# Ten direct pairs instead of eleven, and the transform's work staged around them

## The chip, the cores and the metric

The kernel runs on one core of a Trainium2 chip. The metric is device time in microseconds (us), and for the kernel before it is 1369.09 us, the median of three runs (1367.53 to 1373.18).

## The reference, cut to what matters

```python
S, D, Df = 2048, 576, 4608          # one sequence, all float32
x = A_x
g = sigmoid((x * gate_w).sum(-1, keepdims=True))            # one gate per token
X = rfft2(x); a = irfft2(X * (w_r + 1j * w_i), s=(S, D))    # over tokens and features
h = gelu(x @ w_gate) * (x @ w_up)                           # 576 -> 4608, tanh form
b = h @ w_down                                              # 4608 -> 576
return g * a + (1 - g) * b
```

Both branches work on the same x. All is float32: a product is made of three reduced-precision products (high by high, low by high, high by low parts).

## The kernel before, in words

**The dense branch sets the pace on TensorE (PE).** The 2048 tokens are two halves of 1024. The hidden width 4608 is 36 blocks of 128, two of which make a pair, so there are 18 pairs for each half, 36 in all. The string `PLAN` (L35) has one letter for each. A pair "c" (`conv`) is direct: for two hidden blocks, two groups of 512 tokens, gate and up, `chain` (L826) issues 14 matmuls of 512 columns, 8 x 14 = 112 in all. A pair "s" (`products`) takes its four output blocks from seven block products (Strassen's way), each for gate and up: `seven` (L1140) issues 7 matmuls of 512 columns, 7 x 2 x 7 = 98. Both are followed by the same 96 matmuls of 288 columns of the down projection (`down_mm`, L898), 12 for each of 8 token groups.

An "s" pair needs sums of blocks of x (`operands`, tiles `sx`, `xhi`, `xlo` and the third weight buffer `gu_72`) and sums of weight blocks (`total`, L1120, DVE L1128). Each of its weights is copied rounded by ScalarE (ACT, `copy`, L218), and the rest of it is made by VectorE (DVE, L1111). The first product's result is copied into a second bank of PSUM by ACT, `copy(ps[1][s], v)` in `products`, and the second product is added there: so the second product waits for those two copies.

PSUM has three kinds of banks, two of each: `pgu` and `pone` for the 512-column results and `pdn` for the down projection. `bank` (L844) chooses by a counter, `turns`, which starts at 0: two chains take `pone`, then two `pgu`, and so on. The very first two chains (`first_chains`, L849) always take both `pone`.

**The transform branch** is a generator, `spectral` (L652). Its work is put between matmuls: after each chain or product `gap` (L727) lets it emit as many DVE instructions as the PE time issued since then pays for. Every engine executes its own list strictly in the order of emission. So what stands early in DVE's list and waits for a transfer holds up what stands behind it, though that may be wanted by PE.

The stages are: operands for the first "s" phase; the feature transforms of half one (`forward_rows`, in the tile `rows`, 128 x 5120), stored to DRAM as `fw`, and of half two, both during the first "s" pairs; during the direct pairs the token transform, in the tile `til`, which is the same memory as `sx` (hence the direct pairs): moves from rows to tiles, a stage over tiles (`first_tiles`, with factors), 16 column blocks (`columns`, with 192 matmuls of 290 columns, L283, and exchanges of half tiles by DMA, `hx` and `til`, L269 to L273), and the inverse stage (`last_tiles`); then `operands` again; then during the second "s" phase the inverse feature transforms (`inverse_rows`) whose results are added to the output in DRAM (`yd`). At the end of the direct pairs half one is moved to rows directly (`into_rows`) and half two is stored to DRAM (`bw`) and fetched later (`fetch`, `fetched_rows`). A pair that begins an "s" phase waits until the operands are done; the last pair of all waits until the generator is.

Gates: `gate_sum` (L754) sums x times gate_w, `release` (L949) scales the first four results, which wait in `til`, by one minus the gate.

All SyncE (SP) DMAs stand in one list too.

Of the kernel before, what the change touches and what calls it, by code (L numbers as in the profile page):

```python
# [34 lines left out]
PLAN = "c" * 2 + "s" * 10 + "c" * 11 + "s" * 13  # L35
# [126 lines left out]
def _build(nc, tc, a):  # L162
    with ExitStack() as ctx:
# [42 lines left out]
        bw = dram.tile([P, 8 * SW], F32, name="bw", tag="bw")  # L206
# [32 lines left out]
        def columns():  # L239
# [3 lines left out]
            ww = [[b[:, SW * i:SW * (i + 1)] for i in range(2)] for b in (tmp[:, SW:3 * SW], misc)]  # L243
# [153 lines left out]
        def first_tiles(h):  # L397
            T = tiles()
            sp = tmp[:, 0:2 * SW].rearrange("p (e k) -> p e k", e=2)
            tmps = [tmp[:, SW * i:SW * (i + 1)] for i in range(4)]  # L400
            tmps = [(x, x[:, 0:NK], x[:, NK:]) for x in tmps]
            e = slice(2 * h, 2 * h + 2)
            yield from _butterfly(vec, lambda i: T[:, i, e], lambda i: T[:, i, e, re], lambda i: T[:, i, e, im],
                                  TAKEN, sp, -1, (1.28, 0.69))
# [5 lines left out]
        def last_tiles():  # L410
            T = tiles()
            rows = rows_tile()
            sp = rows[:, 0:4 * SW].rearrange("p (e k) -> p e k", e=4)
            tmps = [rows[:, SW * i:SW * (i + 1)] for i in range(4, 8)]
            tmps = [(x, x[:, 0:NK], x[:, NK:]) for x in tmps]
            places = [((k, LEFT[o]), o * k) for k in range(1, 4) for o in range(1, 4)]
# [3 lines left out]
            yield from _butterfly(vec, lambda i: T[:, i], lambda i: T[:, i, :, re], lambda i: T[:, i, :, im],  # L420
                                  range(4), sp, 1, (2.5, 1.28))
# [164 lines left out]
        def load_rows(rows, h):  # L586
            v = rows.rearrange("p (c g k) -> p c g k", c=2, g=4)
            nc.sync.dma_start(v[:, 0], a["xn"][h, :, :, 0:OW])
            nc.sync.dma_start(v[:, 1, :, 0:2 * D - OW], a["xn"][h, :, :, OW:])
            pl.memset(v[:, 1, :, 2 * D - OW:], 0.0)  # L590

        def with_gates(work):
# [6 lines left out]
            for v in work:  # L599
                yield v  # L600
                n += 1
                t = n // 10 - 1
                if n % 10 == 0 and t < 8:
# [16 lines left out]
        def fetch(b):  # L620
            for i, o in enumerate(spots_of[b]):
                g, c = divmod(i, 2)
                t = 4 * b + 2 * g
                nc.sync.dma_start(o, bw.rearrange("p (t c k) -> p t c k", t=8, c=2)[:, t:t + 2, c])

        def fetched_rows():

            rows = rows_tile()
# [3 lines left out]
            for b in range(2):  # L632
                for i, x in enumerate(spots_of[b]):
# [7 lines left out]
                if b == 0:  # L641
                    yield None
                    fetch(1)
# [5 lines left out]
        pairs_of += [misc[:, 0:SW], misc[:, SW:]]  # L649
        spots_of = [[x.rearrange("p (t k) -> p t k", t=2) for x in pairs_of]] * 2  # L650

        def spectral(rows):  # L652
            for i in (2, 1):
                load_part(0, i)
            for _ in range(2):
                yield None
            yield from operands(0)
            yield from with_gates(forward_rows(0, rows))
# [820 lines left out]
```

## Time and profile before

| | |
|---|---|
| median, lowest and highest of 3 runs | 1369.09, 1367.53, 1373.18 us |
| the profiled execution's own time | 1368.03 us |
| its span in the trace | 1366.1 us |
| PE, DVE, ACT, POOL busy | 1344.1, 1104.2, 833.0, 264.5 us |
| matmuls | 7364 |

The span runs from the first to the last instruction of the trace; 1.9 us of the profiled execution lie outside it. Times in the timeline are from the span's start. [...] In rows of the timeline the bracket at the end is the idle time of the engine before that row and what ended it.

### The profile page before, as it was taken

The page shows a single profiled execution, that of the slowest core. Times are in us where ns is not written, and L with a number is a line of the kernel's source. Part 1 is how long each engine was busy: PE and PEld are TensorE (multiplying, and loading weights), DVE is VectorE, ACT ScalarE, POOL GpSimd, SP SyncE. Part 2 cuts the span into 40 slices and gives each one's busy share as a digit, 9 for nine tenths or more (in the row PEclk, how much of TensorE's full clock was granted, in tenths as well). Part 3 has the DMA queues.
Part 4 walks back from the last instruction along what each step waited for, and adds up shares of the span by engine and source line. Part 5 has one row for each costly group of instructions (what it writes and reads, how often), then busy time and mean ns, then how long its engine had stood idle before and what let it go on. Part 6 is the DMA issues. An engine that isn't in the chain of part 4 may idle for free.

```text
span 1366.1 us, 19980 instructions
## 1 busy us (share of the span) xinstructions
PE 1344.1 (98%) x7364; PEld 1185.5 (87%) x7364; DVE 1104.2 (81%) x1543; ACT 833.0 (61%) x1428; POOL 264.5 (19%) x323
## 2 busy tenths in 40 slices
PE   8999999999999999999999999999999999999998
PEld 6878888888888888898888888878888888888887
DVE  6689989959999878768688587379999579999654
ACT  4676676656665544555566537556766776676672
POOL 0011212212212212222120122111222322221231
PEclk9999999999999999999999999999999999999999
DMA  8556766787667967999996687556767796676897
GB/s 303 186 126 156 146 127 125 149 229 137 127 120 157 196 128 176 200 226 237 259 243 208 178 181 165 88 137 125 133 130 130 137 225 124 126 140 128 148 215 175
DMA packets 107921, 226.92 MB, mean 166 GB/s; under 512 B 12720, under 2 KB 25008, under 8 KB 107696
## 3 DMA queue, kind: packets, MB, share of 16 engines
q0 software_dynamic: 44928, 90.98, 44.4%
q1 hardware_dynamic: 62896, 134.68, 30.5%
q8 instruction: 57, 0.93, 0.3%
q14 instruction: 40, 0.33, 0.1%
HBM read 121.46 MB, written 97.01 MB: 160 GB/s over the span
## 4 chain that ended last, share of the span: by engine, by line
PE 79%; DMA 8%; DVE 7%; ACT 3%; issue 2%; SPq 1%; DVEq 0%; ACTq 0%
PE pdn L906 27%; PE pgu L1146 5%; PE pone L1146 5%; PE pgu L1148 5%; PE pgu L1147 5%; PE pone L1148 5%; PE pone L1147 5%; PE pgu L831 3%; PE pgu L833 3%; PE pgu L832 3%; DMA hx<-til 3%; PE pgu L1149 2%; PE pone L1149 2%; PE pone L831 2%; PE pone L833 2%
## 5 line engine op out<-in xcount | busy, mean ns | idle before, releaser
L919 POOL DMA_DIRECT2D yd<-stg x264 | 229.6, 871 | 1029.7 <-ACT stg L931 838.4
L906 PE MATMUL pdn<-dn,hb 128*128 128x288 f32 x2508 | 364.9, 295 | 1.4 <-DVE dn L810 1.0
L906 PEld LDWEIGHTS pdn<-dn,hb 128*128 128x128 f32 x2508 | 352.3, 188 | 13.9 <-DVE dn L810 1.2
L931 ACT ACTIVATE stg<-pdn,omg 128x576 f32<-128x576 f32 x276 | 204.0, 740 | 246.3 <-PE pdn L906 241.8
L218 ACT ACTIVATE gu<-wq 64x256 fp32r<-64x256 f32 (+4 forms) x353 | 230.1, 666 | 92.2 <-DVE gu L1111 58.7
L1111 DVE TENSOR_TENSOR gu<-wq,gu 128x768 fp32r<-128x768 f32 x161 | 153.6, 955 | 39.9 <-ACT gu L218 37.1
L906 PE MATMUL pdn<-dn,hx 128*128 128x288 f32 x924 | 142.9, 295 | 0.5 <-DVE wq L970 0.2
L906 PEld LDWEIGHTS pdn<-dn,hx 128*128 128x128 f32 x924 | 132.1, 188 | 4.9 <-DVE wq L970 0.5
L831 PE MATMUL pgu<-xhi,gu 128*128 128x512 f32 x296 | 115.9, 392 | 1.2 <-DVE gl L888 1.2
L833 PE MATMUL pgu<-xlo,gu 128*128 128x512 f32 x296 | 115.8, 391 | 0.0
L832 PE MATMUL pgu<-xhi,gu 128*128 128x512 f32 x296 | 115.6, 390 | 0.0
L1128 DVE TENSOR_TENSOR wq<-wq 128x768 f32<-128x768 f32 x92 | 87.5, 953 | 5.0 <-ACT gu L218 4.8
L218 ACT ACTIVATE hb<-gl 128x512 fp32r<-128x512 f32 x68 | 42.7, 628 | 55.5 <-DVE gl L888 53.3
L833 PEld LDWEIGHTS pgu<-xlo,gu 128*128 128x128 f32 x296 | 55.6, 188 | 12.6 <-DVE xlo L776 0.4
L831 PEld LDWEIGHTS pgu<-xhi,gu 128*128 128x128 f32 x296 | 55.6, 188 | 11.6 <-DVE gl L888 1.9
L832 PEld LDWEIGHTS pgu<-xhi,gu 128*128 128x128 f32 x296 | 55.6, 188 | 9.6
L810 DVE TENSOR_TENSOR dn<-wq,dn 128x576 fp32r<-128x576 f32 x72 | 54.4, 756 | 7.6 <-ACT dn L218 7.5
L888 DVE TENSOR_TENSOR gl<-gl,pgu 128x512 f32<-128x512 f32 x37 | 25.3, 684 | 42.5 <-PE pgu L838 42.3
L1146 PE MATMUL pgu<-xhi,gu 128*128 128x512 f32 x140 | 55.6, 397 | 2.6 <-ACT pgu L218 2.6
L1146 PE MATMUL pone<-xhi,gu 128*128 128x512 f32 x136 | 54.1, 398 | 3.1 <-ACT pone L218 3.0
L1146 PE MATMUL pgu<-sx,gu 128*128 128x512 f32 x140 | 55.0, 393 | 1.7 <-DVE gl L1167 1.7
L1147 PE MATMUL pgu<-xhi,gu 128*128 128x512 f32 x140 | 55.2, 394 | 0.0
(242 smaller groups left out, 2844.9 us busy)
## 6 DMA issues: line engine op xcount, KB each, us to landing
yd<-stg POOLq DMA_DIRECT2D x264, 288.0 KB, 4.9
wq<-ws SPq DMA_DIRECT2D x92, 384.0 KB, 4.4
wq<-wd SPq DMA_DIRECT2D x72, 288.0 KB, 5.0
wq<-wgu SPq DMA_DIRECT2D x24, 640.0 KB, 6.1
colm<-col POOLq DMA_DIRECT2D x32, 256.0 KB, 6.4
tmp<-wf SPq DMA_DIRECT2D x16, 290.0 KB, 6.5
hx<-til SPq DMA_DIRECT2D x64, 72.5 KB, 5.8
til<-hx SPq DMA_DIRECT2D x64, 72.5 KB, 3.6
```

The lines of the kernel that those rows point to most:

```text
L218: act.activation(o, i, AF.Copy)
L831: pe.matmul(ps, w[:, 0, k, c], xhi[tb][:, k], start=k == 0, stop=False)
L832: pe.matmul(ps, w[:, 1, k, c], xhi[tb][:, k], start=False, stop=False)
L833: pe.matmul(ps, w[:, 0, k, c], xlo[tb][:, k], start=False, stop=False)
L906: pe.matmul(ps[half], h[:, l, c], d[:, k, half * HD:(half + 1) * HD], start=part == 0 and n == 0, stop=part == 1 and n == 2)
L919: pl.dma_start(yd[u], o, accum_op=ALU.add)
L931: put(u, lambda o: act.activation(o.rearrange("p (c k) -> p c k", c=2), v[:, :, 0:HD], AF.Copy, scale=omg[:, u:u + 1]), i == 0)
L1111: vec.tensor_tensor(o, x.rearrange("p (c k) -> p c k", c=3), f(w[:, 256:1024]).rearrange("p (c k) -> p c k", c=3), ALU.subtract)
L1128: at(lead, lambda: vec.tensor_tensor(o, u, v, ALU.subtract))
L1146: pe.matmul(ps, hi, xh[:, t], start=start and t == 0, stop=False, skip_group_check=True)
L1147: pe.matmul(ps, lo, xh[:, t], start=False, stop=False, skip_group_check=True)
L1148: pe.matmul(ps, hi, xl[:, t], start=False, stop=False, skip_group_check=True)
```

## The change

- The third letter group of `PLAN` goes from 11 to 10 "c" pairs and the last from 13 to 14 "s".
- `turns` starts at 1, so the first `chain` takes a `pgu` bank.
- `total` of an "s" phase's first two weight sums is emitted five gaps after the first weights of that phase, not at the end of the last direct pair.
- At the start 9 idle matmuls instead of 6, the first cast of x ahead of the first weight remainder; the first half of the second weight block is loaded ahead of `msk`, and `sgn` later. The eight gate sums of half one go two to a gap, and `spectral` starts with the releases, after its first loads.
- Half two's rows for the transform come as nine blocks (`xm`): six are loaded into small tiles while half one is transformed (`ahead`), three into `rows` later. The store of `fw` is two DMAs instead of four.
- `first_tiles` and `last_tiles` are cut (two parts, two halves); the column stage's first exchanges are issued between the parts.
- Both halves of the inverse go to DRAM (`bw`, twice as large) and come back by `fetch` and `fetched_rows`; `into_rows` isn't called.

```diff
-PLAN = "c" * 2 + "s" * 10 + "c" * 11 + "s" * 13
+PLAN = "c" * 2 + "s" * 10 + "c" * 10 + "s" * 14
...
             yield from four(0, TAKEN, sp, -1)
+            load_ww(0)
+            yield None
+            for kb in range(2):
+                corner(kb, 0, False)
+            n = 0
+            for v in first_tiles(0, 1):
+                yield v
+                n += 1
+                if n == 10:
+                    for kb in range(2):
+                        corner(kb, 0, True)
+            cols[0] = True
             side.append(beside())
-            load_ww(0)
-            for back in range(2):
-                for kb in range(2):
-                    corner(kb, 0, back)
-                for _ in range(4):
-                    yield None
...
-        def forward_rows(h, rows):
+        def forward_rows(rows, src=None):
             x = blocks(rows, ROW_BLOCK)
+            src = src or x
...
-                yield from nine(((tA, q, 1, s), (q, q, -1, s), (s, p, 1, tA), (p, tA, -0.5, p)))
+                u, v, w = src[i], src[i + 3], src[i + 6]
+                yield from nine(((tA, v, 1, w), (q, v, -1, w), (s, u, 1, tA), (p, tA, -0.5, u)))
...
+        ahead = [misc[:, 0:TB], misc[:, SW:SW + TB], out_rows[3][:, 0:TB], tmp[:, 1536:2048], tmp[:, 2048:2560], gl[1]]
+        def load_block(o, i):
+            nc.sync.dma_start(o, a["xm"][:, i].rearrange("p (g w) -> p g w", g=4))
...
-        def fetched_rows():
+        def fetched_rows(h):
+            for _ in range(5 if h == 0 else 0):
+                yield None
...
-            for b in range(2):
-                for i, x in enumerate(spots_of[b]):
+            for b in range(1 if h == 0 else 2):
+                for i, x in enumerate(places_of[h]):
...
         def spectral(rows):
             for i in (2, 1):
                 load_part(0, i)
-            for _ in range(2):
+            for u in range(4):
+                while len(kept_rows) <= u:
+                    yield None
+                release(u)
                 yield None
...
-            yield from quarters(lambda c: nc.sync.dma_start(fw[:, c], rows[:, c]))
-            for _ in range(2):
+            for c in range(2):
+                nc.sync.dma_start(fw[:, 2 * UNIT * c:2 * UNIT * (c + 1)], rows[:, 2 * UNIT * c:2 * UNIT * (c + 1)])
+            for _ in range(4):
                 yield None
             rows = rows_tile()
-            load_rows(rows, 1)
-            for _ in range(6):
-                yield None
-            yield from forward_rows(1, rows)
+            src = [None] * 9
+            for o, i in zip(ahead, (0, 3, 6, 1, 4, 7)):
+                src[i] = o
+            for i in (5, 2, 8):
+                load_block(x[i], i)
+                src[i] = x[i]
+            yield None
+            yield None
+            yield from forward_rows(rows, src)
...
-            yield from last_tiles()
-            yield None
-            for i in range(4):
-                c = slice(2 * SW * i, 2 * SW * (i + 1))
-                nc.sync.dma_start(bw[:, c], til[0][:, 8 * SW:][:, c])
-                yield None
-            yield from into_rows(0)
-            yield from operands(1)
+            yield from last_tiles(1)
+            yield from with_stores(last_tiles(0), kept(1))
+            yield from with_stores(operands(1), kept(0))
             yield from until(3)
-            fetch(0)
+            fetch(0, 0, places_of[0])
+            yield from fetched_rows(0)
             yield from inverse_rows(0)
-            yield from fetched_rows()
+            yield from fetched_rows(1)
             yield from inverse_rows(1)
...
-        turns = [0]
+        turns = [1]
...
                     prep_b(q + 1, 0)
                     prep_b(q + 1, 1, 2)
+                    at(5, lambda: [total(q + 1, 0), total(q + 1, 1)])
...
-                if tb == 1 and last:
-                    total(q + 1, 0)
-                    total(q + 1, 1)
...
-        for _ in range(6):
+        for _ in range(9):
             pe.matmul(ps, idle[:, 0:P], idle, start=True, stop=True)
```

How the order on the engines moves, at three places.

PE, at the start, from the end of the first two chains (before, then after; `pone` and `pgu` are the PSUM banks that are written):

```order
L857 MATMUL pone<-xlo_65,gu_71 128x512 x2
L857 MATMUL pone<-xtl_67,gu_71 128x512 x4
L831 MATMUL pone<-xhi_63,gu_72 128x512
L832 MATMUL pone<-xhi_63,gu_72 128x512
L833 MATMUL pone<-xlo_65,gu_72 128x512
```

```order
L903 MATMUL pone<-xlo_65,gu_71 128x512 x2
L903 MATMUL pone<-xtl_67,gu_71 128x512 x4
L877 MATMUL pgu<-xhi_63,gu_72 128x512
L878 MATMUL pgu<-xhi_63,gu_72 128x512
L879 MATMUL pgu<-xlo_65,gu_72 128x512
```

The third chain no longer writes a bank that the first two chains have just filled.

DVE, around the start of the second "s" phase (`gl_83<-gl_83,pgu` is gate times up of the last direct chain, `hb` the remainder of its rounding, `wq<-wq 128x768` the weight sums, `gu` the weights' remainders):

```order
L1111 TENSOR_TENSOR gu_70<-wq,gu_70 128x3x256 x2
L888 TENSOR_TENSOR gl_83<-gl_83,pgu 128x512
L892 TENSOR_TENSOR hb_78<-gl_83,hb_78 128x512
L1128 TENSOR_TENSOR wq<-wq 128x768 x2
L1111 TENSOR_TENSOR gu_71<-wq,gu_71 128x3x256
L96 TENSOR_TENSOR tmp<-rows 128x1280
```

```order
L1160 TENSOR_TENSOR gu_71<-wq,gu_71 128x3x256 x2
L1177 TENSOR_TENSOR wq<-wq 128x768 x2
L934 TENSOR_TENSOR gl_83<-gl_83,pgu 128x512
L938 TENSOR_TENSOR hb_78<-gl_83,hb_78 128x512
L1160 TENSOR_TENSOR gu_70<-wq,gu_70 128x3x256
L1177 TENSOR_TENSOR wq<-wq 128x768
```

The two weight sums stand ahead of the last chain's results instead of behind them.

DVE, at the first instructions of half two's forward transform (`tmp` and `rows` of lines 437 to 441, and 446 to 450 of the changed kernel, are the transform; the others serve the "s" pairs):

```order
L1111 TENSOR_TENSOR gu_70<-wq,gu_70 128x3x256
L437 TENSOR_TENSOR tmp<-rows 128x512
L439 TENSOR_TENSOR rows<-rows 128x4x128
L1128 TENSOR_TENSOR wq<-wq 128x768
L437 TENSOR_TENSOR rows<-rows,tmp 128x4x128
L441 SCALAR_TENSOR_TENSOR rows<-tmp,rows 128x4x128
```

```order
L1233 TENSOR_TENSOR xraw<-xraw,pgu 128x512
L446 TENSOR_TENSOR tmp<-misc,orow 128x512
L448 TENSOR_TENSOR rows<-misc,orow 128x4x128
L1233 TENSOR_TENSOR xraw<-xraw,pgu 128x512
L1160 TENSOR_TENSOR gu_71<-wq,gu_71 128x3x256
L446 TENSOR_TENSOR rows<-misc,tmp 128x4x128
L450 SCALAR_TENSOR_TENSOR rows<-tmp,misc 128x4x128
```

The first of these read small tiles that were loaded ahead, not `rows`.

More of the change, by code (lines that the diff above doesn't have):

```diff
@@ L242, in columns @@
             vs = tmp[:, 0:SW]
-            ww = [[b[:, SW * i:SW * (i + 1)] for i in range(2)] for b in (tmp[:, SW:3 * SW], misc)]
+            ww = [[b[:, SW * i:SW * (i + 1)] for i in range(2)] for b in (misc, tmp[:, SW:3 * SW])]
             turn = [d + 4 * q for d in range(4) for q in range(4)]
@@ L692, in spectral, with kept, with_stores @@
             load_xs(1)
-            yield from last_tiles()
-            yield None
-            for i in range(4):
-                c = slice(2 * SW * i, 2 * SW * (i + 1))
-                nc.sync.dma_start(bw[:, c], til[0][:, 8 * SW:][:, c])
-                yield None
-            yield from into_rows(0)
-            yield from operands(1)
+            def kept(h):
+                yield None
+                for i in range(4):
+                    c = slice(8 * SW * h + 2 * SW * (3 - i), 8 * SW * h + 2 * SW * (4 - i))
+                    nc.sync.dma_start(bw[:, c], til[0][:, c])
+                    yield None
+            def with_stores(work, stores):
+                for n, v in enumerate(work):
+                    if n % 2:
+                        next(stores, None)
+                    yield v
+                yield from stores
+            yield from last_tiles(1)
+            yield from with_stores(last_tiles(0), kept(1))
+            yield from with_stores(operands(1), kept(0))
             yield from until(3)
-            fetch(0)
+            fetch(0, 0, places_of[0])
+            yield from fetched_rows(0)
             yield from inverse_rows(0)
-            yield from fetched_rows()
+            yield from fetched_rows(1)
             yield from inverse_rows(1)
@@ L1345, in _build @@
         one, fin = gate_part(0, rows0, gwb)
-        for t in range(8):
-            aux.append(lambda t=t: one(t))
+        for t in range(0, 8, 2):
+            aux.append(lambda t=t: [one(t), one(t + 1)])
         aux.append(fin)
-        for u in range(0, 4, 2):
-            aux.append(lambda u=u: [release(u), release(u + 1)])
         aux.append(lambda: gens.append(spectral(rows0)))
```

87 lines of the change are left out of this document (52 added, 35 removed).

## The prediction, made before the changed kernel was run

> **What bounds the kernel now.** I read the page's busy times first, then the list of waits of PE, then PE's timeline and the windows around each wait.
>
> ```profile
> PE 1344.1 (98%) x7364; PEld 1185.5 (87%) x7364; DVE 1104.2 (81%) x1543; ACT 833.0 (61%) x1428; POOL 264.5 (19%) x323
> ...
> 893.08 0.39 PE L1147 MATMUL pgu<-xhi,gu 128*128 128x512 f32 x1
> ...
> 895.80 0.39 PE L1149 MATMUL pgu<-sx,gu 128*128 128x512 f32 x1
> ```
>
> PE is busy 98% of the span, and from 893.08 to 895.80 there are 12 steps of one matmul each: 2.72 / 12 = 0.227 us. That is the pace of a 512-column matmul when nothing is waited for. So time can come from two places alone: fewer matmuls, or shorter waits of PE. These are its waits:
>
> ```profile
> PE pone L1146 <- ACT pone L218: 3.0, 1, 3.0
> PE pgu L1146 <- ACT pgu L218: 2.6, 1, 2.6
> PE pone L831 <- ACT gl L878: 2.3, 1, 2.3
> PE pgu L1146 <- DVE gl L1167: 1.7, 1, 1.7
> PE pgu L831 <- DVE gl L888: 1.2, 1, 1.2
> PE pone L283 <- ACT til L218: 1.1, 1, 1.1
> PE pone L283 <- DVE colm L276: 0.9, 1, 0.9
> ```
>
> These seven are 12.8 us; no other inside the span's first and last few us is above 1.0. The three longest cost more than they show, because the clock goes down behind them:
>
> ```profile
> 12.00:15.38 3.38, 1.53 (x7) 0.94 (x5) 2.38 (x4) 2.85 (x5) 0.00 (x0) 1.00 1.03 367
> 15.38:18.80 3.41, 2.98 (x7) 2.41 (x8) 2.20 (x4) 2.05 (x4) 0.00 (x0) 0.54 1.01 346
> 83.65:87.06 3.41, 0.81 (x4) 0.35 (x2) 3.38 (x6) 3.09 (x6) 0.00 (x0) 1.00 0.69 152
> 87.06:90.47 3.41, 3.38 (x8) 2.65 (x9) 3.38 (x6) 0.94 (x3) 0.00 (x0) 0.54 0.00 1
> 896.02:899.43 3.41, 0.40 (x2) 0.23 (x2) 2.42 (x3) 2.34 (x4) 0.00 (x0) 1.00 0.67 227
> 899.43:902.85 3.41, 3.41 (x10) 2.61 (x10) 3.41 (x4) 1.15 (x4) 0.00 (x0) 0.54 0.00 0
> ...
> 300.00:310.00 10.00, 8.27 (x43) 6.83 (x42) 9.48 (x14) 5.90 (x10) 1.03 (x2) 1.00 0.51 106
> ```
>
> The first number after the comma is PE's busy time, the third from the end the granted clock. In three stretches of 3.4 us PE works for 1.53, 0.81 and 0.40 us, and in the stretch behind each the clock is 0.54. The wait of 1.7 us near 305 (last row) left it at 1.00.
>
> [...]
>
> **The change, part by part.**
>
> *One direct pair less.* 112 matmuls of 512 columns become 98: 14 x 0.227 = **3.2 us less**. The down projection and the 192 column matmuls stay. The planner inserts no idle gap for a late operand in the changed program, so all of it should be seen.
>
> *The third chain's bank.*
>
> ```profile
> 12.46 1.07 PE L857 MATMUL pone<-xtl,gu 128*128 128x512 f32 x4
> 15.81 0.79 PE L831 MATMUL pone<-xhi,gu 128*128 128x512 f32 x1 [2.28 <-ACT gl L878]
> ...
> 12.09 0.74 ACT L218 ACTIVATE gu<-wq 128x640 fp32r<-128x640 f32 x1 [1.53 <-DMA wq<-wgu]
> ...
> 13.94 1.33 ACT L218 ACTIVATE xhi<-til 128x512 fp32r<-128x512 f32 x2 [0.16 <-DMA til<-xt]
> 15.18 0.58 ACT L878 ACTIVATE gl<-pone 128x512 f32<-128x512 f32 x1
> ```
>
> PE waited for the Gelu that empties `pone`; the Gelu stood behind two copies of x that waited for DMA. With a `pgu` bank the chain needs only weights that were ready at 12.83 (12.09 + 0.74). The wait of 2.28 goes. So does the half clock: in the window of 0.54 seven matmuls ran from 15.81 to 18.80, where 2.99 / 0.227 = 13 fit, so 6 x 0.227 = 1.4 are lost there. Together **3.7 us less**. Bounds: 0 if the next group of tokens is late in its place; 3.7 if nothing is. I take 3.7, because x's copies end at 15.27 and the two chains between take 28 x 0.227 = 6.4 us from 13.5.
>
> *Nine idle matmuls.*
>
> ```profile
> 1.46 2.93 PE L1322 MATMUL pgu<-hb 128*128 128x512 f32 x6 [1.46 <-DVE gate L1318]
> 5.22 2.04 PE L857 MATMUL pone<-xhi,gu 128*128 128x512 f32 x4 [0.84 <-DVE xhi L1329]
> ```
>
> At about 0.45 us each, three more fill the 0.84 us of waiting and add 0.5 to it, while the cast of x moves forward by one DVE instruction (0.42). Bounds +0.5, and -1.0 if the clock rises sooner: the four matmuls at 5.22 take twice the 1.07 of those at 12.46. I take -0.3.
>
> *The weight sums, sooner.* Here the second "s" phase starts:
>
> ```profile
> 893.06 0.69 DVE L888 TENSOR_TENSOR gl<-gl,pgu 128x512 f32<-128x512 f32 x1 [2.33 <-PE pgu L838]
> 894.45 0.69 DVE L892 TENSOR_TENSOR hb<-gl,hb 128x512 fp32r<-128x512 f32 x1 [0.70 <-ACT hb L218]
> 895.05 1.94 DVE L1128 TENSOR_TENSOR wq<-wq 128x768 f32<-128x768 f32 x2
> ...
> 893.78 0.63 ACT L218 ACTIVATE hb<-gl 128x512 fp32r<-128x512 f32 x1 [2.57 <-DVE gl L888]
> 897.09 1.58 ACT L218 ACTIVATE gu<-wq 128x768 fp32r<-128x768 f32 x2 [2.68 <-DVE wq L1128]
> 898.57 1.06 ACT L218 ACTIVATE pone<-pgu 128x512 f32<-128x512 f32 x2
> ...
> 899.20 0.50 PE L1146 MATMUL pone<-xhi,gu 128*128 128x512 f32 x1 [3.01 <-ACT pone L218]
> ...
> 903.20 0.39 PE L1146 MATMUL pone<-xhi,gu 128*128 128x512 f32 x1
> ```
>
> PE wants the copies `pone<-pgu`. In ACT's list they stand behind two weight copies, which wait 2.68 us for the sums, and the sums stand in DVE's list behind the last chain's results. With the sums ahead of L888 (the order on DVE shows it, and DVE was idle for 2.33 us there) ACT goes on at 894.41: two weight copies (1.58) to 895.99, the first PSUM copy (half of 1.06) to 896.5. PE is through with its 14 matmuls at 895.80 + 0.23 = 896.03, so 0.5 remains of 3.01. From 899.20 to 903.20 are ten steps, 4.00 us where 2.27 would do: 1.7 for the clock. Together 2.5 + 1.7 = **4.2 us less**. Bounds: 0, and 4.7.
>
> The first "s" start is the same with another cause:
>
> ```profile
> 83.76 0.68 DVE L888 TENSOR_TENSOR gl<-gl,pgu 128x512 f32<-128x512 f32 x1
> ...
> 80.90 0.39 PE L838 MATMUL pgu<-xtl,gu 128*128 128x512 f32 x1
> ...
> 84.47 0.63 ACT L218 ACTIVATE hb<-gl 128x512 fp32r<-128x512 f32 x1 [0.32 <-DVE gl L888]
> ```
>
> The chain ended at 81.29, but DVE came to its result at 83.76, 2.5 us late, behind work on operands that ACT had finished late; the 2.6 us of PE's wait are that. In the changed order the sums stay ahead of L888, so the early sums don't help here. What does are the operands: their loads go before the releases, the gate sums take half the gaps, and the planner has them done two gaps before the pair, where it had to force one gap at the pair's start. Two gaps are two chain parts of 7 matmuls, 7 x 0.227 = 1.6 us each: 3.2 us sooner against 2.5 us late. I take 2.2 of the 2.6, and the clock: eight of the 15 matmuls that fit 3.41 us ran, 7 x 0.227 = 1.6. Together **3.8 us less**, bounds 0 and 4.2.
>
> *Half two's rows staged ahead.*
>
> ```profile
> 300.35 0.69 DVE L437 TENSOR_TENSOR tmp<-rows 128x512 f32<-128x512 f32 x1 [6.91 <-DMA rows<-xn]
> ```
>
> DVE stood still for 6.91 us, and PE's wait of 1.7 for L1167 follows from it. The store of `fw` still has to land before `rows` is written, but it is followed by three blocks of nine, not by the whole load, and the first instruction reads other tiles. I take **1.2 us less** (bounds 0 and 1.7). The bytes are the same.
>
> *Both halves through DRAM.* 4 more stores and 8 more fetches take the place of a copy on ACT and DVE at equal counts. Eight fetches are issued where the second "s" phase starts. The one such fetch before:
>
> ```profile
> DVE rows L637 <- DMA xlo<-bw: 4.7, 1, 4.7
> ```
>
> cost DVE 4.7 us, and none of PE's listed waits follows from it. Bounds 0 and 3 (three groups at 1.0); I take **+1.0**.
>
> *The middle, shorter by a pair.*
>
> ```profile
> 600.00:700.00 100.00, 96.76 (x537) 84.77 (x536) 75.78 (x123) 59.92 (x103) 22.58 (x31) 1.00 1.02 251
> ...
> 800.00:900.00 100.00, 96.99 (x526) 85.23 (x526) 58.24 (x73) 55.72 (x89) 17.91 (x21) 1.00 0.65 134
> ```
>
> DVE, the third number, is busy for 76 and 58 of 100 us there. The place that goes with the pair (a tenth to an eleventh of the direct pairs' time, under 40 us) is less than DVE's idle time of 66 us in these two stretches alone. PE's waits of the column stage (1.2, 1.1 and 0.9 in the list) will fall elsewhere: I leave their sum, with +-4 for the range. The halves of `last_tiles` add ten DVE instructions beside PE.
>
> **Sum:** -3.2 - 3.7 - 0.3 - 4.2 - 3.8 - 1.2 + 1.0 = -15.4. Of the profiled execution's 1368.03 us (its span of 1366.1 and 1.9 around it, which stay) that leaves 1352.6. The median of the three runs, 1369.09, lies 1.1 above that execution, so I forecast **1353.7 us** (own range 1348 to 1359).
>
> **Rivals.**
>
> *The starts keep their waits.* If DVE or ACT are late at both "s" starts as before, now from denser work ahead of them (the operands stand next to `last_tiles`), their 4.2 + 3.8 = 8.0 us stay: 1361.7. For it: the first start's remedy is only 0.7 us longer than what it must cure. Against: 2.33 us of idle DVE at the second. Chance 0.12.
>
> *New waits in the middle.* Every term above comes true, but the transfers that fill the DMA engines at 1.02 now meet a column stage that is issued earlier, and PE loses some 10 us more there, as if each of the 16 blocks waited two thirds of the 0.9 in the list: 1363.7. Chance 0.09.
>
> *Slower.* The exchanges `til<-hx` decide: ACT waited for them
>
> ```profile
> ACT colm L218 <- DMA til<-hx: 17.2, 6, 6.5
> ```
>
> in six cases, 2.9 us each, and PE lost 1.1 in the dearest of its waits for a block (L283). If each of the 16 blocks cost PE 1.1 us and the half clock behind it (1.4), 40 us come on top: 1394. From 1.0 us a block on the gain of 15.4 is gone, from 1.4 the kernel is slower by over 0.5%. Against it: the 600 to 700 window has the same reload of x and kept PE at 97%. Chance 0.05.
>
> *Only the pair counts.* The waits are taken over by whatever comes second in each list; 3.2 us: 1365.9. Chance 0.05.
>
> *The clock stays low.* The stretches at 0.54 have another cause than the waits ahead of them and stay when these go: 1.4 + 1.7 + 1.6 = 4.7 us less gain, 1358.4. Against it: each of the three stands right behind a long wait, and no other row shows such a clock. Chance 0.04. [...]
>
> My forecast has 0.65.
>
> **The numbers.** A difference of 0.5%, 6.8 us, is about what a measurement of this kernel can tell, so faster means below 1362.2. Forecast and low clock are (0.69), and of the kept waits most (0.09): 0.78. Same: the rest of that, the middle and the lone pair, 0.03 + 0.09 + 0.05 = 0.17. Slower 0.05. The range reaches down by the middle's waits (4), the fetches at nothing (1.0), the idle matmuls at their better end (0.7) and the staged rows at theirs (0.5), 6 us together with some room, and up over the kept waits and the middle: 1347 to 1365.
>
> **What would show it.** 7353 matmuls (14 fewer, 3 idle more). No wait of L877, the third chain. At both "s" starts waits below 0.6, and a clock of 1.00 in the windows behind them. DVE's wait for half two's rows below 2 us, and no PE wait of 1.7 there. Waits of PE for fetches below 1. I am wrong if a column block's matmul (L283) waits often, or DVE holds a fetched row's instruction for longer than 5 us with PE idle behind it.

## The result and the profile after

The changed kernel took 1354.62 us (median; 1353.12 to 1356.02) beside 1368.61 us for the kernel before: a ratio of 0.9891, 95% interval 0.9866 to 0.9917. The forecast was 1353.7. Measured once more beside the last experiments it took 1358.53 us (1353.68 to 1362.38), ratio 0.9921 (0.9893 to 0.9950). The gain is 11 to 14 us where 15.4 were forecast. The first profiled execution has a span of 1352.0 us, 14.1 less than before; the second has 1360.6.

Busy times of the changed kernel, and the head of its list of waits of PE (in total, how many, the longest; below these rows are 0.8, 0.6 and 0.2):

```profile
PE 1335.8 (99%) x7353; PEld 1180.6 (87%) x7353; DVE 1112.5 (82%) x1566; ACT 839.3 (62%) x1446; POOL 263.3 (19%) x323
```

```profile
PE pone L283 <- DVE colm L276: 3.1, 2, 2.4
PE pgu L1195 <- ACT pgu L218: 2.7, 3, 1.6
PE pgu L877 <- DVE gl L934: 2.2, 2, 1.2
PE pgu L1372 <- DVE gate L1368: 1.5, 1, 1.5
```

Three of the four longest waits of before are gone: the third chain's for its bank, the second "s" start's 3.0, and the 1.7 for L1167 near 305. What is left sits at the first "s" start (1.6) and in the column stage (L283, L934), where it has grown: 5.3 us in four waits (3.1 + 2.2), against 4.2 in four before (2.0 for L283, 1.2 for L888 and 1.0 for down weights, L906, between them). The row of 2.7 also holds a wait of 0.9 near 358 that the kernel before does not have; e_rows_late and e_rows_spread below do not have it either, and its cause is open. These are PE's own rows at the third chain and at the two "s" starts:

```profile
13.41 0.39 PE L877 MATMUL pgu<-xhi,gu 128*128 128x512 f32 x1
...
82.05 0.50 PE L1195 MATMUL pgu<-xhi,gu 128*128 128x512 f32 x1 [1.61 <-ACT pgu L218]
...
852.44 0.50 PE L1195 MATMUL pgu<-xhi,gu 128*128 128x512 f32 x1 [0.22 <-ACT pgu L218]
```

And the windows (PE's busy time after the comma, the granted clock third from the end), at the first "s" start and in the column stage:

```profile
79.40:82.82 3.42, 1.80 (x8) 1.20 (x7) 2.67 (x4) 3.40 (x6) 0.00 (x0) 1.00 0.13 24
82.82:86.23 3.41, 3.41 (x16) 2.81 (x15) 3.38 (x6) 1.96 (x4) 0.00 (x0) 1.00 0.00 0
...
686.97:690.39 3.42, 1.29 (x7) 0.89 (x5) 2.50 (x5) 0.82 (x2) 0.00 (x0) 1.00 1.11 333
690.39:693.80 3.41, 3.12 (x9) 2.75 (x10) 2.04 (x4) 3.04 (x6) 0.57 (x1) 0.54 0.92 269
```

One half clock (a window granted 0.54) is left of three, and it stands behind a wait (2.42 us, for a column block) that the kernel before did not have.

### The profile page after: what moved, and what is told of

Read it like the earlier page. It is cut to its first block, busy times and chain, and to the rows that moved or that the text cites. A ratio compares the mean times of both kernels' runs of the same rounds, so it can differ in the third digit from the quotient of the medians.

```text
span 1352.0 us, 20022 instructions
## 1 busy us (share of the span) xinstructions
PE 1335.8 (99%) x7353; PEld 1180.6 (87%) x7353; DVE 1112.5 (82%) x1566; ACT 839.3 (62%) x1446; POOL 263.3 (19%) x323
## 4 chain that ended last, share of the span: by engine, by line
PE 91%; ACT 2%; DVE 2%; DMA 2%; issue 1%; SPq 0%; DVEq 0%; ACTq 0%
PE pdn L952 32%; PE pgu L1195 6%; PE pgu L1197 6%; PE pgu L1196 6%; PE pone L1195 6%; PE pone L1197 5%; PE pone L1196 5%; PE pgu L877 4%; PE pgu L879 4%; PE pgu L878 4%; PE pgu L1198 3%; PE pone L1198 3%; PE pone L877 2%; PE pone L879 2%; PE pone L878 2%; PE pone L283 1%
## 5 line engine op out<-in xcount | busy, mean ns | idle before, releaser
L952 PE MATMUL pdn<-dn,hb 128*128 128x288 f32 x2472 | 361.2, 295 | 0.3 <-DVE wq L1019 0.2
L952 PEld LDWEIGHTS pdn<-dn,hb 128*128 128x128 f32 x2472 | 347.7, 188 | 13.4 <-ACT stg L978 0.7
L218 ACT ACTIVATE gu<-wq 64x256 fp32r<-64x256 f32 (+4 forms) x365 | 236.1, 661 | 75.7 <-DVE gu L1160 54.3
L1160 DVE TENSOR_TENSOR gu<-wq,gu 128x768 fp32r<-128x768 f32 x168 | 159.7, 952 | 33.4 <-ACT gu L218 33.0
L952 PE MATMUL pdn<-dn,hx 128*128 128x288 f32 x960 | 148.3, 295 | 0.0
L952 PEld LDWEIGHTS pdn<-dn,hx 128*128 128x128 f32 x960 | 137.4, 188 | 4.1
L877 PE MATMUL pgu<-xhi,gu 128*128 128x512 f32 x276 | 108.7, 394 | 2.2 <-DVE gl L934 2.2
L878 PE MATMUL pgu<-xhi,gu 128*128 128x512 f32 x276 | 108.3, 392 | 0.0
L879 PE MATMUL pgu<-xlo,gu 128*128 128x512 f32 x276 | 108.2, 392 | 0.0
L1177 DVE TENSOR_TENSOR wq<-wq 128x768 f32<-128x768 f32 x96 | 91.2, 952 | 10.7 <-ACT gu L218 10.2
L856 DVE TENSOR_TENSOR dn<-wq,dn 128x576 fp32r<-128x576 f32 x72 | 54.1, 752 | 10.8 <-ACT dn L218 10.7
L877 PEld LDWEIGHTS pgu<-xhi,gu 128*128 128x128 f32 x276 | 52.2, 189 | 11.6 <-DVE gl L934 3.0
L878 PEld LDWEIGHTS pgu<-xhi,gu 128*128 128x128 f32 x276 | 52.1, 189 | 8.5
L1195 PE MATMUL pgu<-xhi,gu 128*128 128x512 f32 x144 | 56.8, 394 | 2.7 <-ACT pgu L218 2.7
L1195 PE MATMUL pone<-xhi,gu 128*128 128x512 f32 x144 | 56.6, 393 | 0.1
L1195 PE MATMUL pgu<-sx,gu 128*128 128x512 f32 x144 | 56.5, 392 | 0.0
L1195 PE MATMUL pone<-sx,gu 128*128 128x512 f32 x144 | 56.4, 392 | 0.0
L1197 PE MATMUL pgu<-xlo,gu 128*128 128x512 f32 x144 | 56.2, 391 | 0.0
```

The lines of the kernel that those rows point to most:

```text
L218: act.activation(o, i, AF.Copy)
L877: pe.matmul(ps, w[:, 0, k, c], xhi[tb][:, k], start=k == 0, stop=False)
L878: pe.matmul(ps, w[:, 1, k, c], xhi[tb][:, k], start=False, stop=False)
L879: pe.matmul(ps, w[:, 0, k, c], xlo[tb][:, k], start=False, stop=False)
L952: pe.matmul(ps[half], h[:, l, c], d[:, k, half * HD:(half + 1) * HD], start=part == 0 and n == 0, stop=part == 1 and n == 2)
L1160: vec.tensor_tensor(o, x.rearrange("p (c k) -> p c k", c=3), f(w[:, 256:1024]).rearrange("p (c k) -> p c k", c=3), ALU.subtract)
```

## The experiments

The third column is the time of the kernel before, run beside each. Kernels in rows with the same figure there ran side by side and are compared with each other.

| kernel | us | before beside it | ratio, 95% interval |
|---|---|---|---|
| e_bank_old | 1359.03 | 1368.85 | 0.9925 (0.9905 to 0.9946) |
| e_sums_old | 1362.75 | 1368.85 | 0.9950 (0.9934 to 0.9966) |
| e_plan_alone | 1366.16 | 1368.85 | 0.9988 (0.9971 to 1.0004) |
| e_copy_first | 1353.74 | 1368.85 | 0.9897 (0.9877 to 0.9917) |
| e_eleven | 1377.14 | 1366.80 | 1.0069 (1.0045 to 1.0093) |
| e_half_direct | 1352.92 | 1366.80 | 0.9907 (0.9893 to 0.9920) |
| e_rows_late | 1363.77 | 1366.80 | 0.9982 (0.9967 to 0.9997) |
| e_both | 1347.00 | 1366.80 | 0.9856 (0.9843 to 0.9868) |
| e_late | 1350.26 | 1369.48 | 0.9860 (0.9831 to 0.9890) |
| e_both11 | 1365.93 | 1369.48 | 0.9976 (0.9956 to 0.9996) |
| e_rows_spread | 1356.62 | 1369.48 | 0.9902 (0.9866 to 0.9938) |
| c_after (the changed kernel again) | 1358.53 | 1369.48 | 0.9921 (0.9893 to 0.9950) |

### The third chain's bank

```
-        turns = [1]
+        turns = [0]
```

> The changed kernel with the bank counter back at 0, so the third chain writes a bank that the first two have just filled. Theory (the bank was the wait): a PE wait of about 2.2 us before the third chain, a stretch of 3.4 us at a clock near 0.54 behind it, and 3.7 us more than the changed kernel, about 1358.3 us. Rival (the start is paced by the transfers that bring the first tiles, and PE would catch up with them anyway): under 1 us more, and a wait of about the same length later in the first 40 us of the changed kernel; its trace shows none there.

Measured: 1359.03 us. PE's list has the wait back, for the same Gelu as before:

```profile
PE pone L877 <- ACT gl L924: 1.7, 1, 1.7
```

No half clock followed in this execution:

```profile
13.14:16.56 3.42, 1.73 (x8) 1.14 (x7) 2.63 (x4) 2.36 (x5) 0.00 (x0) 1.00 1.02 390
16.56:19.97 3.41, 3.41 (x17) 2.83 (x16) 2.01 (x4) 2.60 (x6) 0.00 (x0) 1.00 0.96 365
```

So the bank's wait is shown. Its clock part did not come in this execution: the wait is 1.7 here and PE still worked for 1.73 us in its window, where the kernel before had 2.3 and 1.53. By time the term cannot be sized: the ratio lies inside the interval of the changed kernel's second measurement.

### The weight sums

```
-                    at(5, lambda: [total(q + 1, 0), total(q + 1, 1)])
...
+                if tb == 1 and last:
+                    total(q + 1, 0)
+                    total(q + 1, 1)
```

> The changed kernel with the two weight sums emitted at the end of the last direct pair as before. Theory (ACT's weight copies stand behind the sums and hold up the PSUM copies): at the second start PE waits about 3 us instead of 0.2, with a half-clock stretch behind it, 4.3 us more; at the first start, where the sums now also fall behind the last chain's results, about 2.5 to 3 us instead of 1.6, and the clock too, 2 to 3 us more: 1361 us. Rival (the second start's wait went because operands finish seven gaps earlier, not because of the sums): no change at the second start, 1355 us.

Measured: 1362.75 us. The waits for the PSUM copies rise from 2.7 to 7.4:

```profile
PE pgu L1195 <- ACT pgu L218: 7.4, 4, 3.4
```

3.4 of it is the first "s" start and 3.0 the second, which has two half windows behind it (granted 0.54 and 0.50):

```profile
859.88:863.29 3.41, 1.42 (x7) 0.84 (x5) 2.41 (x4) 1.09 (x2) 0.00 (x0) 1.00 1.07 321
863.29:866.70 3.41, 2.39 (x6) 1.90 (x7) 3.35 (x4) 1.78 (x4) 0.00 (x0) 0.54 0.98 337
866.70:870.12 3.42, 3.42 (x10) 2.65 (x9) 0.00 (x0) 2.20 (x4) 0.00 (x0) 0.50 0.21 54
```

So the early sums carry both starts. The prediction gave them the second alone, and said that at the first they don't help. This execution (1369.28 us) is the slowest of its ten, its mean clock is 0.993 (0.998 in the changed kernel's first execution), and 7.9 us of waits in the column stage are in it too, so the time of the sums is not read from it.

### The pair alone, in the kernel before

```
-PLAN = "c" * 2 + "s" * 10 + "c" * 11 + "s" * 13
+PLAN = "c" * 2 + "s" * 10 + "c" * 10 + "s" * 14
```

> The kernel before with nothing changed but ten direct pairs between and 14 block products behind. Theory (the matmuls saved are 3.2 us, and the staging is what makes room for them): the planner emits five gaps without a matmul at the second start, PE idles 5 to 10 us there in place of 3.0, with the half clock behind: 1368 to 1373 us, no gain. Rival (the pair alone brings what it saves, the rest is for the waits): 1365.5 us.

Measured: 1366.16 us, 2.7 less than before and near the rival's 1365.5; the interval just reaches 1. The longer waits at the second "s" start and at L1167 are there in the profiled execution, one of the slowest of its ten (1370.7 us):

```profile
PE pgu L1146 <- ACT pgu L218: 8.9, 2, 5.9
PE pgu L1146 <- DVE gl L1167: 4.3, 1, 4.3
```

The time doesn't bear out the 1368 to 1373 that I drew from the forced idle steps; how many of its executions have these waits isn't known. In its column stage, with ten direct pairs, PE's waits are 3.4 us.

### The eleventh pair put back into the changed kernel

The same line, the other way round (`"c" * 11 + "s" * 13`).

> The changed kernel with eleven direct pairs and 13 as block products, all else as in it: 14 more matmuls of 512 columns, and the last stage of operands one pair later against the second "s" start, where the planner now inserts 14 idle steps. Theory (the pair is worth its 14 matmuls): +3.2 us against the changed kernel, 1357.8. Rival (what the pair gave was spent in the middle again: the column stage's waits of PE, 5.4 us in the changed kernel against 3.2 before, come from the shorter middle): these waits fall to about 3 and the time stays near 1355. Second rival (the operands are late at the second start): a wait of 2 to 3 us there with a half clock behind it, 1362.

Measured: 1377.14 us, slower than the kernel before, and 18.6 and 22.5 us over the changed kernel's two medians where 3.2 were expected. Its waits:

```profile
PE pdn L952 <- ACT hb L218: 6.3, 1, 6.3
PE pone L1195 <- ACT pone L218: 6.2, 2, 6.0
PE pone L283 <- DVE colm L276: 5.8, 2, 5.4
PE pgu L877 <- DVE gl L934: 4.0, 2, 2.9
```

None of the three readings held. The first rival wanted the column stage's waits down to about 3; with a longer middle they are 9.8 us. That is no more than the changed kernel itself can show (10.8 in c_after below), so the length of the middle is not shown to matter for them either way. And two waits came up, of L952 at 824 and of L1195 at 1321, where the changed kernel's first execution has none above 0.2. They are taken up again under e_both11.

### Half one straight to the rows

```
-            yield from with_stores(operands(1), kept(0))
+            yield from into_rows(0)
+            yield from operands(1)
...
-            fetch(0, 0, places_of[0])
-            yield from fetched_rows(0)
+            fetch(1, 0, places_of[1])
```

> The changed kernel with half one's last tiles copied straight into the rows in the middle, as the kernel before did it, and only the other half fetched from DRAM; the operands of the second "s" phase then end just where the phase starts, and not seven gaps earlier. Theory: DVE and ACT are late at the second "s" start, PE's wait of 2 to 3 us comes back there with the half clock, +4 us against the changed kernel, 1358.6. Rival (the way of half one's rows doesn't matter to PE): within 1 us of it, 1354.6, and no wait above 0.6 at the second start. The prediction's term was +1.0 for the fetches; if they cost that, this kernel is 1 us faster.

Measured: 1352.92 us, 1.7 under the changed kernel, less than the two measurements of that kernel differ. The waits for PSUM copies are 3.9 in all against 2.7, since the second "s" start waits again:

```profile
PE pgu L1195 <- ACT pgu L218: 3.9, 3, 1.6
```

The wait came as the theory said, at about half its size (1.4), and the time stayed with the rival. The mean clock is 0.998, as in the changed kernel's first execution; the half window here (0.54 from 710.03) is in the column stage. So the way through DRAM gives some slack at the second start, and the time does not tell the two ways apart. Where it costs is seen below.

### Half two's rows late, in one gap and in three

In both kernels no block is staged ahead. e_rows_late issues all nine in one gap, e_rows_spread three in each of three gaps.

```
-            for i in (5, 2, 8):
+            for i in (0, 3, 6, 1, 4, 7, 5, 2, 8):
                 load_block(x[i], i)
...
-            yield from forward_rows(rows, src)
+            yield from forward_rows(rows)
```

> The changed kernel with half two's nine blocks loaded into the rows where the kernel before loaded them, behind the store of the first half, none staged ahead. Theory: DVE waits about 7 us again for the rows, and PE's wait of 1.7 for the Gelu's result behind them is back: +1.2 to 1.9 us, 1356.2. Rival: DVE's wait is back but something else covers it in the changed kernel, no wait of PE above 1 there, 1354.6.

Measured: 1363.77 us. PE's worst wait in the list is not the 1.7 for a Gelu's result:

```profile
PE pdn L947 <- DVE hx L1214: 8.7, 1, 8.7
```

On DVE and on SP's queue (the second column is the duration) stands why:

```profile
291.01 0.96 DVE L1172 TENSOR_TENSOR wq<-wq 128x768 f32<-128x768 f32 x1 [10.42 <-DMA wq<-ws]
...
277.67 5.14 SPq L607 DMA_DIRECT2D rows<-xm  x4
282.91 2.02 SPq L1140 DMA_DIRECT2D wq<-ws  x1
```

DVE did not wait for the rows but for a weight slice, whose load stands on SP behind the nine; the last four of them took 5.14 us on the queue. The next kernel leaves the rows late and moves the weight slice ahead of six of them:

> The kernel that loads half two's nine blocks late (1363.8 us), with the nine loads issued in three gaps, three in each, and not all in one. Theory (what cost PE 8.7 us there was not the rows but the queue: the weight slice of L1140 was issued on SP behind nine loads, at 282.7 where the changed kernel issues it at 273.8): the weight slice is issued behind three loads again, no PE wait above 2 us near 288, 1356. Rival (DVE is held by the late rows themselves): DVE's wait for rows is 7 us or more and PE waits 4 us or more there, 1361 to 1364.

Measured: 1356.62 us, within the scatter of the changed kernel beside it (1358.53). PE's wait at that place is down to

```profile
PE pdn L948 <- DVE hx L1215: 1.8, 1, 1.8
```

The theory of the queue holds: with the weight slice ahead, late rows leave a wait of 1.8, much as before the change (1.7), behind a DVE that waits 1.8 for the rows themselves; with nine loads ahead of the slice it is 8.7, and the clock is at 0.54, 0.50 and 0.50 in three windows behind it (from 290.96, 294.37 and 297.79).

### The PSUM copies ahead of the weight copies

At both "s" starts `copy(ps[1][s], v)` is issued right behind the product, ahead of the weight copies that the gap emits.

```
-                    seven(v, q, n, name, s, n in (0, 3), n in (1, 5, 6))
+                    first = n == 0 and q in starts
+                    seven(v, q, n, name, s, n in (0, 3), n in (1, 5, 6),
+                          (lambda: copy(ps[1][s], v)) if first else None)
+                    if first:
+                        continue
```

> The changed kernel with the two PSUM copies of the first product at both starts of block products emitted ahead of the weight copies in ACT's list. Theory (PE's remaining wait of 1.6 us at the first start is ACT's order alone): waits of L1195 for ACT at both starts below 0.2 us, 1.7 us less than the changed kernel, 1353 us. Rival (the weight copies, now later, are wanted at the third product): the same wait or more appears one or two products later, 1354.6 us or above.

Measured: 1353.74 us. The start's waits are gone; what is left in this group is mainly the wait of 0.9 near 358 that the changed kernel has as well:

```profile
PE pgu L1195 <- ACT pgu L218: 1.0, 2, 0.9
```

No wait came up one or two products later, as the rival had it. So the first start's 1.6 us goes with the order of ACT's list. That these microseconds do not show in the time led to the column stage, whose waits were 8.6 us in this execution.

### The column stage

In c_after, the changed kernel again, the waits of that stage are 10.8 us where the first execution had 5.3.

> The changed kernel once more, unchanged, beside the others: the time to compare them with on the same chip, and a second profiled execution of the column stage. Theory: 1354.6 within 1.5 us, no waits above 0.6 at the second "s" start, 1.6 at the first, and column waits that differ from the first execution's by up to 2 us.

Measured: 1358.53 us, 3.9 over the first measurement where 1.5 was allowed for; the waits of the two starts came as expected (1.6, and none above 0.6), those of the column stage differ by 5.5 us and not by 2:

```profile
PE pgu L877 <- DVE gl L934: 5.4, 2, 4.4
PE pone L283 <- DVE colm L276: 5.4, 2, 4.7
```

DVE and the windows at the first of them:

```profile
600.89 1.56 DVE L96 TENSOR_TENSOR til<-til 128x580 f32<-128x580 f32 x2 [4.98 <-DMA til<-hx]
602.36 0.68 DVE L934 TENSOR_TENSOR gl<-gl,pgu 128x512 f32<-128x512 f32 x1
...
599.35:602.76 3.41, 0.00 (x0) 0.00 (x0) 1.84 (x3) 0.00 (x0) 0.00 (x0) 1.00 1.06 288
602.76:606.17 3.41, 3.07 (x7) 2.48 (x8) 2.38 (x5) 2.40 (x5) 0.00 (x0) 0.54 0.86 232
```

L96 is a butterfly of the stage's second half (`beside`), on a block that its DMA has not brought back; the DMA engines are full (1.06). Behind it in DVE's list stands L934, the product that PE wants. The edit lets that second half start one block later:

```
-                    while gone[0] < (4 * d + 5) * STEP + 5:
+                    while gone[0] < (4 * d + 6) * STEP + 5:
```

> The changed kernel with one edit alone: the column blocks' second stage may start one block later (the second edit of the 1347.0 us kernel, without the copies issued first). Theory (the column stage holds DVE's and ACT's lists for blocks that have not landed, and the gate gives them time): PE's waits of the column stage fall from 5.4 us to below 2.5 and their half clock goes; the first start's wait of 1.6 stays: 1348.5. Rival (the gain of that kernel comes from both edits together): 1352 to 1354.

Measured: 1350.26 us, 8.3 less than c_after beside it. All waits of the column stage are in one row now:

```profile
PE pone L283 <- DVE colm L276: 1.5, 2, 1.0
PE pdn L952 <- ACT hb L218: 1.8, 1, 1.8
```

DVE comes to the L934 in question without L96 ahead of it:

```profile
594.93 0.69 DVE L934 TENSOR_TENSOR gl<-gl,pgu 128x512 f32<-128x512 f32 x1 [1.16 <-PE pgu L884]
```

The theory holds, 1.8 us above its number: the second row, a wait of 1.8 near 811 with a half clock behind it, is new. With the copies issued first as well:

> The changed kernel with two edits: at both "s" starts the copies of the PSUM results are issued ahead of the weight copies of the same gap, and the column blocks' second stage may start one block later, so that DVE's list is not held by work on a reloaded block that has not landed. Theory: the first start's wait of 1.6 is gone, as in the run with the first edit alone, and PE's waits for the Gelu's product of DVE at the column stage (near 596) are below 1; no half clock there: 1351 to 1353. Rival (the column stage's waits come from the transfers themselves and move with them): as many microseconds of waits at other blocks, 1354 to 1356.

Measured: 1347.00 us (1346.07 to 1347.80), below every one of the changed kernel's ten times (the lowest 1353.12), and faster than both kernels; its theory gave 1351 to 1353. Over e_late alone its ratio is not proved better (0.9856 against 0.9860).

```profile
PE pone L283 <- DVE colm L276: 1.2, 2, 1.0
PE pdn L952 <- ACT hb L218: 1.2, 1, 1.2
```

### The eleventh pair once more, without the column stage's waits

e_both with `"c" * 11 + "s" * 13`.

> The 1347.0 us kernel with eleven direct pairs and 13 as block products. The changed kernel alone lost 22 us by that step, 3.2 of them for 14 matmuls, the rest in three places: the column stage, a wait of 6.3 us for the last tiles' fetch near 824, and one of 6.0 at the forced idle steps near 1321. Theory (three separate causes): the column stage's loss goes, the other two with their half clocks stay: 1347 + 3.2 + 8 + 8 = 1366. Rival (all three follow from the column stage being late): 1350 to 1352.

Measured: 1365.93 us. Two waits carry it:

```profile
PE pone L1195 <- ACT pone L218: 6.9, 1, 6.9
PE pdn L952 <- ACT hb L218: 5.9, 1, 5.9
```

and on ACT, ahead of them:

```profile
811.10 1.15 ACT L218 ACTIVATE sx<-tmp 128x512 fp32r<-128x512 f32 x2 [12.62 <-DMA bw<-til]
...
1311.51 0.86 ACT L592 ACTIVATE tmp<-rows,gs 128x640 f32<-128x640 f32 x1 [4.54 <-DMA yd<-tmp]
```

The first of these rows is in the operands of the second "s" phase, ahead of the 5.9; the other in the last stage, where ACT waits for an output store before it refills `tmp`, ahead of the PSUM copies that PE wants. Theory and time agree (1366): these two are separate from the column stage. The spans of e_both11 and e_both differ by 18.7 us (1364.3 and 1345.6): 3.2 for the matmuls, 5.9 - 1.2 = 4.7 and 6.9 for the two waits; the rest, 3.9, is put down to the two half windows behind each of the two (0.54 and 0.50, from 813.43 and from 1311.78), an estimate. By the ratios of all their executions the step is 16.4 us. Why one more direct pair makes these two stages late is not shown.

**The first of the two is the true price of "both halves through DRAM".** `sx` is the same memory as `til`, so the operands of the second "s" phase cannot be written before the stores of the last tiles to `bw` have landed. ACT's row for it, in the changed kernel, e_late and e_eleven:

```profile
ACT sx L218 <- DMA bw<-til: 6.5, 1, 6.5
```

```profile
ACT sx L218 <- DMA bw<-til: 8.6, 1, 8.6
```

```profile
ACT sx L218 <- DMA bw<-til: 13.0, 1, 13.0
```

PE's wait there is none, 1.8 and 6.3: ACT's wait less 6.7. e_both, e_both11 and c_after fit (8.0, 12.6 and 7.1 on ACT; 1.2, 5.9 and 0.4 on PE). In these six executions, and within 0.1 in the five others that have this wait, up to 6.7 us of it are covered; above, each microsecond is PE's. The kernel before and e_half_direct have no such wait of ACT.

## Why the prediction was right, and where it was not

By its own steps, with what the two profiled executions show (a half window at 0.54 is 3.41 x 0.46 = 1.6 us):

| term | forecast | first execution after |
|---|---|---|
| one pair less | -3.2 | -3.2 by count |
| bank and idle matmuls | -4.0 | -3.8: the third chain starts at 13.41, not 15.81, and 1.4 of clock |
| second "s" start | -4.2 | -4.5: 3.01 becomes 0.22, and 1.7 of clock |
| first "s" start | -3.8 | -2.6: 2.64 becomes 1.61, and 1.6 of clock |
| half two's rows | -1.2 | -1.7 |
| both halves through DRAM | +1.0 | 0 |
| the middle | 0, +-4 | +2.7: waits 5.3 for 4.2, and one half clock |
| sum | -15.4 | -13.1, of 14.1 in the span; 1.0 is in no row |

That the time came within 1 us of the forecast is partly luck. Losses that the sum did not have (2.7 in the middle, 1.2 at the first start) met gains that it did not have (1.0 for the fetches, 0.5 for the rows, and the 1.0 in no row), and measured again the kernel was 4.8 us above the forecast.

- **The bank, the second start and the rows** came out as worked out. That the idle matmuls brought 0.3 isn't shown: without its wait of 2.28 the third chain of before would have started at 13.5.
- **The first "s" start** was mis-sized: 1.0 us of its wait went where I took 2.2. I named the operands as the cure and said that the early sums don't help. It is still the sums that stand ahead of L934, and they wait for ACT:

```profile
76.23 1.95 DVE L1177 TENSOR_TENSOR wq<-wq 128x768 f32<-128x768 f32 x2 [1.26 <-ACT gu L218]
...
78.70 0.68 DVE L934 TENSOR_TENSOR gl<-gl,pgu 128x512 f32<-128x512 f32 x1
...
79.41 0.63 ACT L218 ACTIVATE hb<-gl 128x512 fp32r<-128x512 f32 x1 [2.91 <-DVE gl L934]
79.95 1.56 ACT L218 ACTIVATE gu<-wq 128x768 fp32r<-128x768 f32 x2
81.42 1.06 ACT L218 ACTIVATE pgu<-pone 128x512 f32<-128x512 f32 x2
```

  Put late again the wait is 3.4 (e_sums_old), so the sums do help there. What is left is two weight copies ahead of the PSUM copies on ACT (with the copies first the whole 1.6 goes, e_copy_first), which I had seen at the second start and not asked about at the first.
- **Both halves through DRAM** was priced at the wrong end, the eight fetches. No wait of PE follows from them. The price is at the four stores, and the changed kernel stands 0.2 us on the good side of it in its first execution (6.5 of 6.7) and 0.4 on the bad side in the second.
- **The middle** is the step that failed. That PE's waits of the column stage "will fall elsewhere: I leave their sum" should have been a loss: 2.7 us in the first execution, and 6.6 of waits with two half clocks (0.54 from 602.76 and from 698.33), 9.7 us, in the second. That is the size of the rival "new waits in the middle" (1363.7), which that execution (1362.4) comes near; the second measurement's median lies about halfway between forecast and rival. DVE's share of idle time, on which I rested, was no argument: it is idle there because its list waits (its waits in those two stretches of the kernel before are 26.7 and 41.6 us). e_late shows the mechanism. Which part of the change brought it was not tried. The gate of `beside` is the same line in both kernels. The pair alone did not bring it (3.4 us in e_plan_alone), and putting the pair back did not remove it (9.8 in e_eleven), so the reordered stages are left: most likely the cut of `first_tiles` and the exchanges issued between its parts, which is not shown.
- **The pair**: its 3.2 is right for the matmuls and says little of what the edit is worth. Alone it brought 2.7 or nothing; put back into the improved kernel, the eleventh pair costs 16 to 19, most of it as two waits, for the stores ahead of the operands and in the last stage.
- **The clock** followed the waits, as forecast: in the first execution after it is at 1.00 from 4.55 to 690.63 and from 694.04 to 1349.40, so behind the third chain and both "s" starts. The half window that is left stands behind the window of 686.97 shown above, in which PE was busy for 1.29 us; behind c_after's of 599.35, with PE idle throughout, the clock was 0.54 as well.

## What to carry to other kernels

Price a wait on an engine with a list by its slack: here a store's landing was free up to 6.7 us and cost one for one beyond, so a change that moves a place in time can be worth five to six times its own work (16 to 19 us against 3.2), and a term found by taking an edit away isn't the term of putting it in. Where an engine looks idle beside full DMA queues, see what its list waits for before counting that time as room; an instruction on data still in flight belongs behind the one that PE wants. Ask what a batch of loads stands ahead of on its DMA queue: here the weight slice behind nine loads left at 282.91 (e_rows_late), and in the changed kernel, behind three, at 274.07, 1.8 us after the first of them.

## What the runs showed of the hardware

In the trace of the kernel before, the clock goes down three times behind PE's waits, each time for 3.41 us; these stretches begin 71.7 and 812.4 us apart, which is 21 and 238 times 3.413. The windows shown here of the two first executions, before and after, are laid to end 0.24 us ahead of such a change, so a stretch at 0.50 reads 0.54.

Laid end to end in this way over these two executions, from 8.6 and 4.3 us on, the windows show six falls: behind 1.56, 0.81 and 0.40 us of PE's work (before, from 11.97, 83.65 and 896.02), behind 1.28 (after, from 686.98), and behind 1.43 and 1.38 at the end of each. It did not fall behind any other; the least work in one of those is 1.69 (before, from 305.51) and 1.80 (after, from 79.40). Laid 0.24 us later, so as to end where the clock changes, the six have 1.32, 0.77, 0.47, 1.04, 1.19 and 1.14, and the two still 1.69 and 1.80.

Of the experiments' windows e_bank_old's with 1.73 (above) kept the clock, and e_rows_spread and e_late, each with a wait of 1.8, differ:

```profile
288.97:292.39 3.42, 1.67 (x10) 1.31 (x9) 3.27 (x5) 0.38 (x2) 0.00 (x0) 1.00 0.94 217
292.39:295.80 3.41, 3.41 (x20) 2.94 (x20) 3.34 (x6) 2.08 (x5) 0.86 (x1) 1.00 0.25 31
```

```profile
810.45:813.87 3.42, 1.57 (x10) 1.26 (x9) 1.66 (x4) 3.42 (x7) 0.86 (x1) 1.00 0.83 232
813.87:817.28 3.41, 3.41 (x16) 3.33 (x16) 2.88 (x5) 3.33 (x7) 0.00 (x0) 0.54 0.32 60
```

Behind 1.67 us of work the clock stayed, behind 1.57 it was 0.54. So a wait of 1.8 cost one kernel a half window, about 1.6 us, and another nothing.

Some waits had two or three half windows behind them, others one. Behind a half window in which PE worked for 2.98, 3.38 or 3.41 us (before) or 3.12 us (after) the clock was back; behind one with 2.39 us (e_sums_old, from 863.29), 1.33 and 1.55 (e_both11, from 813.43 and 1311.78), 0.00 and 0.46 (e_rows_late, from 290.96 and 294.37) it stayed at 0.50.

This is a part of why one kernel's executions spread: 1353 to 1362 us for the changed kernel, 1346 to 1348 for e_both, whose profiled execution has a mean clock of 0.999. The two profiled executions of the changed kernel differ by 8.6 us in span, of which 5.5 are waits of the column stage and about 1.6 one more half window; for the others no trace shows it.
